# From the second block on, attention takes all four sequences of a block in one go

## The chip, the cores and the metric

One core of a Trainium2 chip runs one program. The metric is device time in microseconds (us). TensorE (PE) multiplies matrices; PEld is its loading of weights. VectorE (DVE), ScalarE (ACT) and GpSimd (POOL) do elementwise work, and SyncE (SP) issues nearly all transfers.

## The reference

A gated linear attention over 4 sequences, 8 heads and 768 positions feeds two MLPs, one behind the other. All is float32.

```
for c in range(nc):                              # chunks along the sequence
    L = exp(cum[i] - cum[j]) * causal            # decay inside the chunk
    M = einsum('bhin,bhjn->bhij', Cc, Bc) * L    # scores, weighed
    y[:, :, sl] = M @ xc + (Cc @ state) * exp(cum)
    state = decay_full * state + sum_j Bc x xc * decay_from_j
x = y as (4*768 tokens, 256)
x = softplus(x @ w_in) @ w_out                   # 256 -> 2048 -> 256
out = act2(x @ w2_in) @ w2_out                   # 256 -> 2048 -> 256
```

## The kernel before

**Blocks and units.** The kernel cuts the sequence into 6 blocks of 128 positions (c = 0 to 5), and a block into 4 units, one for each sequence (u = 4c to 4c+3). Blocks 1 to 5 are worked pair by pair: units 4c and 4c+1, then 4c+2 and 4c+3. A pair has these jobs, named as in the code, with a job's number being that of the last unit (scores: of the pair):

- rows, load, load_bc (SP): the clipped decays (tile ld), the inputs (u) and the operands of the scores (bc) are fetched. The buffers of rows and load are given back by the pair's out.
- decay (DVE, L1069): a scan along ld. sources (L1077) makes bt from u and ld; cd (L1089) scales u.
- scores (PE, L1104): 16 small products into four PSUM banks, two called y and two called acc.
- weigh (DVE, L1118): ld = scores * ld, four products of 128x256 a pair.
- st (PE, L1172 and L1150): the first half of ld times u, and the state's sums. Both go to the two y banks.
- carry (DVE, L1160) and sm (ACT, L1241): the new state and its copy that PE reads.
- out (PE, L1204 and L1172): the state's share, and the other half of ld times u.
- evac (ACT, L1224) and ready (DVE, L1232): the result goes as a high and a low part (xh, xl) to the MLP's input.

**The MLP.** Tokens go through layer 1 block by block in steps of 128 hidden columns: up (PE, L1262 to L1264, 3 products for each of 2 halves), g (ACT), g_hi (ACT or DVE), g_lo (DVE or POOL, L1372), down (PE, L1398, 6 matmuls into two acc banks). The first few downs are plain float32 (L1386). Each weight is split into a high and a low part before its first use (w0 to w3, w_hi, split_w: tiles wih, wil, woh, wol), mostly on DVE; some low parts and some g_lo are made on POOL. Blocks 4 and 5 of layer 1 (group 0) and all of layer 2 (groups 1 to 3) share products over two blocks: quads of jobs p15, p26, p37 and p4 on PE (L1269 to L1271), of which each waits for one result of ACT or DVE: fork (ACT) between p15 and p26, add1 (DVE) between p26 and p37, add2 (DVE) between p37 and p4.

**The order.** No engine chooses at run time. `program()` lists jobs with costs, due times and buffers, `Jobs.order` puts them into one list by a greedy rule, and each engine runs its jobs in that order. Constants (LAG_1, CHUNK, HASTE, BIAS) and a table (RUSH) shift due times and tie-breaks, so that a changed cost or constant moves jobs all over the program.

Of the kernel before, what the change touches and what calls it, by code (L numbers as in the profile page):

```python
# [14 lines left out]
NB, H, S, D, N = 4, 8, 768, 32, 16  # L15
# [12 lines left out]
class Jobs:  # L28
# [18 lines left out]
    def order(self, slots, begin):  # L47
# [53 lines left out]
        for _ in range(len(jobs)):  # L101
            best = []
            for name in ready:
# [10 lines left out]
            start, _, _, name, engine, got = min(  # L114
                (b for b in best if b[4] == first[4] and b[0] <= first[0] + (PATIENCE if first[0] > EARLY else HASTE)), key=lambda b: (b[1], b[0], b[2])
            )
# [96 lines left out]
def program():  # L213
# [38 lines left out]
    for u in range(NU):  # L252
# [24 lines left out]
        else:  # L277
            add(("sources", u), DVE, 210, needs=[("load", u)] + decay, takes=["bt"])
        if b % 2:
            v = u // 2  # L280
            add(
                ("scores", v), PE, 830 if c else 1270, needs=[("load_bc", v)] + (decay + [("decay", u - 1)] if c else [("scores", v - 1)] * v),
                takes=["y", "y", "acc", "acc"] if c else ["y", "y"] + [("acc", "h")] * 2 if v == 0 else [("h", "acc")] * 4,
                gives=[("load_bc", v)],
            )
        for hg in range(2):
            n = 2 * u + hg
            weighed = [("decay", u, hg), ("sources", u, hg)] if c == 0 else decay + [("sources", u)]

            bank = [("part", ("scores", u // 2), b % 2 * 2 + hg)]  # L290
            if n in WEIGH_POOL:
                add(("copy", u, hg), ACT, 490, needs=[("scores", u // 2)], takes=["g"], gives=bank)
                add(("weigh", u, hg), POOL, 1350, needs=weighed + [("copy", u, hg)], gives=[("copy", u, hg)])
            else:
                add(("weigh", u, hg), DVE, 340 if c else 600, needs=weighed + [("weigh", u, 0)] * hg + [("scores", u // 2)], gives=bank)
        both = [u] if c == 0 else [u - 1, u]
        if c == 0 or b % 2:

            needs = [("weigh", i, hg) for i in both for hg in range(2)] + ([("out", both[0] - 1)] if u else [])
            if c > 0:  # L300
                add(
                    ("st", u), PE, 990, needs=needs + [("sm", u - NB)], takes=["y", "y"], gives=[("sources", i) for i in both],
                )
                add(("carry", u), DVE, 300, needs=[("st", u), ("dec", c)])
                add(("sm", u, 1), ACT, 500, needs=[("carry", u)])
                needs = [("st", u), ("sm", u, 1)] + [("cd", i) for i in both]
# [5 lines left out]
            needs = [("out", u)]  # L312
            if c > 1:
                needs += [("split_w", 0, kind, j) for kind in "io" for j in range(8) if place_of(kind, j) == c]
                needs += [("down", s) for s in range(WHOLE)]
            if c == 1:

                needs += [("w2" if signed(0, kind, SX) else "w3", 0, kind, SX) for kind in "io"]
            due = when(first_step[c, b] - LEAD if c < 2 else min(first_step[c, b] - LEAD, CHUNK * (c - 1) + SPACE * b + SHIFT))
            add(("evac", u), ACT, 490 if c else 420, needs=needs)  # L320
            add(
                ("ready", u), DVE, 610 + 300 * (c < NC - 1) if c else 340, due=due, needs=[("evac", u)],
                gives=[("st", u) if c else ("out", u)] + [("dec", c)] * (b == NB - 1 and c > 0),
            )
# [81 lines left out]
    for s, (m, c, t0, n, fc, m_fc) in enumerate(steps):  # L406
# [102 lines left out]
BIAS_2 = 9000  # L509
# [6 lines left out]
LAG = 1500  # L516
LAG_1 = 6000
LAG_2 = 18000
# [7 lines left out]
RUSH = {  # L526
    ("cd", 6): -2000, ("columns", 1): -2000, ("decay", 2, 1): 16000, ("down", 1): -1000, ("down", 11): -4000,
    ("down", 2): -16000, ("down", 3): -16000, ("evac", 0): -4000, ("load_w", 0, "o", 3): -2000, ("load_w", 0, "o", 6): -16000,
    ("split_w", 0, "i", 1): 16000, ("split_w", 0, "o", 5): 2000, ("w0", 0, "o", 0): 1000, ("w0", 0, "o", 4): 1000,
    ("w1", 0, "o", 3): -2000, ("w3", 0, "i", 2): -8000, ("w3", 0, "i", 5): 16000, ("w3", 0, "o", 6): -16000,  # L530
    ("w_hi", 0, "i", 1): 1000, ("weigh", 0, 1): -2000,
# [8 lines left out]
def tile_kernel(ctx: ExitStack, tc: tile.TileContext, a0, al, bc, ub, w_in, w_out, w2_in, w2_out, out):  # L540
# [46 lines left out]
    def join():  # L587

        assert jobs.start["out", NB - 1] < jobs.start["scores", NB // 2]
# [501 lines left out]
    def cb_t(u, hg):  # L1091
        return buf(*got["scores", u // 2][u % 2 * 2 + hg])

    @job
    def scores(engine, v):

        t = mine("load_bc", v)[0]
# [30 lines left out]
    def y_t(u):  # L1128
# [4 lines left out]
        buf("y", 0)  # L1133
        i = u % 2
        return bufs["pair"][:, :, i * Q:i * Q + Q], None

    def states_t(u, s):
        buf("y", 0)
        return bufs["pair"][:, s, 256:384].rearrange("p (i n) -> p i n", i=2)

    @job
    def st(engine, u):

        intra_turn(u, 0)
        for i in range(2):
            x, bt = parts(u - 1 + i)[0], flat(bt_t(u - 1 + i))
            for p in range(4):
                for s in range(2):
                    r, o = slice(s * HALF, s * HALF + HALF), slice(p * 32, p * 32 + 32)
                    nc.tensor.matmul(  # L1150
                        states_t(u, s)[o, i], bt[r, p * 32:p * 32 + 32], x[r, p * 64:p * 64 + 64], start=False, stop=True,
                        skip_group_check=True,
                    )
# [24 lines left out]
    def intra_turn(u, turn):  # L1178

        for i in (u - 1, u):  # L1180
            for h in range(4):
                for s in range(2):
                    intra(i, (s + turn) % 2 * 4 + h, halves[s], halves[s], turn == 0 and i == u - 1)

    def out_unit(engine, u):
        c, b = divmod(u, NB)
        if c == 0:
# [9 lines left out]
            return  # L1197
        for i in (u - 1, u):
            y, cdt = y_t(i)[0], parts(i)[2]
            for s in range(2):  # L1200
                for p in range(4):

                    r, o = slice(p * 32, p * 32 + 32), p % 2 * 64
                    nc.tensor.matmul(  # L1204
                        y[o:o + 64, p // 2, halves[s]], sm_t[b // 2][s][r, i % 2], cdt[r, halves[s]], start=False,
                        stop=False, skip_group_check=True,
# [5 lines left out]
    def columns_of(c, b):  # L1212

        n, o = (Q, b * Q) if c == 0 else (2 * Q, b * Q - Q)
        y = y_t(b)[0] if c == 0 else bufs["pair"][:, :, 0:n]
        return [y] + [t[c][:, :, o:o + n] for t in (xh, xl)]
# [207 lines left out]
    with tc.manual_schedule():  # L1424
# [106 lines left out]
```

## Time and profile before

| | |
|---|---|
| median of 3 runs | 564.5 us (563.31 to 564.63) |
| profiled execution | 563.84 us, span 561.9 us, clock share of PE 0.998 |
| PE busy | 553.3 us, 98% of the span |
| PE weight loads | 445.4 us, 79% |
| DVE busy | 449.9 us, 80% |
| ACT busy | 385.1 us, 69% |
| POOL busy | 27.6 us, 5% |
| chain that ended last | PE 91%, DVE 4%, DMA 2% |
| fetch of a pair's decays (ld<-clip_z) | 20 of 256 KB, median 4.6 us to landing |

The busy time of an engine is an average over the whole span. In a row of the timeline the first number is the start in us from the span's start, the second how long the row lasted; a row with xN holds N equal instructions.

### The profile page before, as it was taken

Reading aid. Unit: us, or ns where it says so; the run is one execution under the profiler, and the core shown is the slowest. Engines: PE = TensorE matmul, PEld = TensorE weight load, DVE = VectorE, ACT = ScalarE, POOL = GpSimd, SP = SyncE. Lnnn points to the kernel's source line nnn. Section 1 sums busy time; section 2 is a strip of 40 time slices with the busy share of each in tenths; the row PEclk is TensorE's granted clock in tenths of the full one; section 3 lists DMA queues with packets and bytes.
Section 4 is the critical chain, followed back from the end, with each engine's and each line's share of the span. In section 5 each row is a group of like instructions: output and inputs, shape, how many; then the busy total and the mean of one; then the engine's idle time right before and its main releaser. Section 6 shows DMA issues by size and latency. Waiting matters only on the chain.

```text
span 561.9 us, 10574 instructions
## 1 busy us (share of the span) xinstructions
PE 553.3 (98%) x4070; PEld 445.4 (79%) x4070; DVE 449.9 (80%) x841; ACT 385.1 (69%) x706; POOL 27.6 (5%) x34
## 2 busy tenths in 40 slices
PE   9899999999999999999999999999999999999997
PEld 4767898777778888788888788788788888888885
DVE  6899976687896899877897999967976665876664
ACT  6977744445555666756657887886787785777873
POOL 4030300000000100000100000200100000000000
PEclk9999999999999999999999999999999999999999
DMA  8986541658445003578847132103200001000002
GB/s 283 389 225 187 157 118 31 196 171 225 119 149 178 0 2 93 214 237 304 275 142 240 59 118 90 56 6 108 76 0 1 0 1 38 37 1 0 1 1 76
DMA packets 34679, 64.74 MB, mean 115 GB/s; under 512 B 3684, under 2 KB 8164, under 8 KB 34628
## 3 DMA queue, kind: packets, MB, share of 16 engines
q1 hardware_dynamic: 34628, 64.06, 35.3%
q8 instruction: 32, 0.52, 0.4%
q14 instruction: 19, 0.16, 0.1%
HBM read 47.61 MB, written 16.43 MB: 114 GB/s over the span
## 4 chain that ended last, share of the span: by engine, by line
PE 91%; DVE 4%; DMA 2%; ACT 1%; SPq 1%; issue 1%; DVEq 0%; ACTq 0%
PE acc L1398 44%; PE h L1262 5%; PE h L1269 4%; PE h L1263 4%; PE h L1264 4%; PE h L1271 4%; PE h L1270 4%; PE z L1269 4%; PE z L1271 4%; PE z L1270 4%; PE y L1172 2%; DMA st<-in_w_out_dram 2%; PE acc L1386 1%; PE y L1204 1%; PE y L1104 1%
## 5 line engine op out<-in xcount | busy, mean ns | idle before, releaser
L1372 DVE TENSOR_TENSOR gl<-g,gh 128x512 fp32r<-128x512 f32 x184 | 126.5, 692 | 51.3 <-PE acc L1398 35.4
L1398 PE MATMUL acc<-gh,woh 128*128 128x512 f32 (+1 forms) x384 | 148.9, 390 | 0.0
L1398 PE MATMUL acc<-gh,wol 128*128 128x512 f32 (+1 forms) x384 | 146.5, 384 | 0.0
L683 ACT CAST gh<-g 128x512 fp32r<-128x512 f32 x155 | 96.1, 620 | 32.2 <-PE acc L1398 18.4
L1398 PE MATMUL acc<-gl,woh 128*128 128x512 f32 (+1 forms) x384 | 115.1, 383 | 0.0
L1398 PEld LDWEIGHTS acc<-gh,woh 128*128 128x128 f32 x384 | 72.1, 188 | 16.1 <-issue 1.2
L1398 PEld LDWEIGHTS acc<-gh,wol 128*128 128x128 f32 x384 | 72.2, 188 | 13.5 <-DVE wol L916 0.2
L1398 PEld LDWEIGHTS acc<-gl,woh 128*128 128x128 f32 x384 | 70.9, 188 | 14.4
L1357 ACT ACTIVATE g<-h 128x512 f32<-128x512 f32 x65 | 38.7, 595 | 56.2 <-PE h L1264 41.3
L1349 ACT ACTIVATE t<-t 128x512 f32<-128x512 f32 x96 | 60.8, 634 | 1.9
L1262 PE MATMUL h<-xh,wih 128*128 128x512 f32 (+1 forms) x130 | 48.5, 373 | 0.0
L1263 PE MATMUL h<-xh,wil 128*128 128x512 f32 (+1 forms) x130 | 46.6, 358 | 0.7 <-DVE wil L916 0.7
L1264 PE MATMUL h<-xl,wih 128*128 128x512 f32 (+1 forms) x130 | 46.3, 356 | 0.0
L1263 PEld LDWEIGHTS h<-xh,wil 128*128 128x128 f32 x130 | 24.5, 189 | 4.8 <-DVE wil L916 1.1
L1069 DVE TENSOR_TENSOR_SCAN ld<-ld,eye_t 128x512 f32<-128x512 f32 x20 | 25.8, 1326 | 3.2 <-DMA ld<-clip_z 3.2
L1262 PEld LDWEIGHTS h<-xh,wih 128*128 128x128 f32 x130 | 24.5, 189 | 4.5 <-issue 0.4
L1264 PEld LDWEIGHTS h<-xl,wih 128*128 128x128 f32 x130 | 24.5, 189 | 3.6
L1342 ACT ACTIVATE t<-h 128x512 f32<-128x512 f32 x37 | 22.1, 597 | 7.6 <-PE h L1271 6.0
L1361 DVE TENSOR_TENSOR g<-h,t 128x512 f32<-128x512 f32 x37 | 25.3, 684 | 1.8 <-ACT t L1349 0.8
L1361 DVE TENSOR_TENSOR g<-z,t 128x512 f32<-128x512 f32 x35 | 23.8, 683 | 1.5 <-ACT t L1349 0.8
L1342 ACT ACTIVATE t<-z 128x512 f32<-128x512 f32 x35 | 20.9, 596 | 5.5 <-PE z L1271 3.2
L1322 DVE TENSOR_TENSOR dec_plain<-h,dec_plain 128x512 f32<-128x512 f32 x22 | 15.1, 688 | 7.8 <-PE h L1271 7.6
(321 smaller groups left out, 1004.2 us busy)
## 6 DMA issues: line engine op xcount, KB each, us to landing
st<-in_w_in_dram SPq DMA_DIRECT2D x15, 512.0 KB, 4.0
st<-in_w_out_dram SPq DMA_DIRECT2D x15, 512.0 KB, 4.2
u<-in_ub_dram SPq DMA_DIRECT2D x24, 256.0 KB, 5.5
ld<-clip_z SPq DMA_DIRECT2D x20, 256.0 KB, 4.6
bc<-in_bc_dram SPq DMA_DIRECT2D x12, 384.0 KB, 7.9
pre_i<-st_plain SPq DMA_DIRECT2D x14, 256.0 KB, 3.6
pre_o<-st_plain SPq DMA_DIRECT2D x12, 256.0 KB, 3.7
pre_s<-st_plain SPq DMA_DIRECT2D x14, 192.0 KB, 4.0
```

The lines of the kernel that those rows point to most:

```text
L683: nc.scalar.copy(out, in_)
L1262: nc.tensor.matmul(o, wh, xh[c][:, k, t0:t0 + n], start=(k == 0), stop=False)
L1263: nc.tensor.matmul(o, wl, xh[c][:, k, t0:t0 + n], start=False, stop=False)
L1264: nc.tensor.matmul(o, wh, xl[c][:, k, t0:t0 + n], start=False, stop=(k == 1))
L1269: nc.tensor.matmul(bank, wh, bh, start=start, stop=False, skip_group_check=True)
L1270: nc.tensor.matmul(bank, wl, bh, start=False, stop=False, skip_group_check=True)
L1271: nc.tensor.matmul(bank, wh, bl, start=False, stop=True, skip_group_check=True)
L1342: nc.scalar.activation(out=t, in_=ph, func=act_funcs.IDENTITY_SAT240, scale=SAT)
L1349: nc.scalar.activation(out=t, in_=t, func=AF.Square, scale=0.5 / SAT, bias=0.5)
L1361: nc.vector.tensor_tensor(out=g, in0=ph, in1=t, op=ALU.max)
L1372: engines[engine].tensor_tensor(out=mine("g_lo", s)[0], in0=mine("g", s)[0], in1=mine("g_hi", s)[0].bitcast(F32), op=ALU.subtract)
L1398: nc.tensor.matmul(acc_t(s, e), w, g[:, j * n:(j + 1) * n], start=(begins(e, j) and g is gh and i == 0), stop=(fc + j == NFC - 1 and g is ...
```

## The change

With TOGETHER = (1, 2, 3, 4, 5), blocks 1 to 5 no longer go pair by pair. One scores job computes both pairs, the second into the other half of the same four banks. One st job holds the half products of all four units and the state sums of both pairs, the latter in two acc banks, since y now holds the outputs of four units. One out job follows. Every matmul, every weigh, carry, sm, evac and ready stays, on the same shapes. The buffers of ld and u of all four units are held until that one out, so the next block's rows and loads are issued after it. bt has four buffers in place of three. LAG_1 makes the downs of group 0 due later, and CHUNK, HASTE, BIAS, STAND_BY and RUSH are new numbers for the order.

```diff
+def units_of(u):
+
+    c = u // NB
+    return [u] if c == 0 else list(range(NB * c, NB * c + NB)) if c in TOGETHER else [u - 1, u]
...
-        if b % 2:
+        both = units_of(u)
+        n_pairs = len(both) // 2
+        if u == both[-1] and b % 2:
             v = u // 2
+            pairs = [v - 1, v] if n_pairs == 2 else [v]
             add(
-                ("scores", v), PE, 830 if c else 1270, needs=[("load_bc", v)] + (decay + [("decay", u - 1)] if c else [("scores", v - 1)] * v),
+                ("scores", v), PE, 200 + 630 * n_pairs if c else 1270,
+                needs=[("load_bc", i) for i in pairs] + ([("decay", i) for i in both[:2]] if c else [("scores", v - 1)] * v),
...
-                    ("st", u), PE, 990, needs=needs + [("sm", u - NB)], takes=["y", "y"], gives=[("sources", i) for i in both],
+                    ("st", u), PE, 200 + 790 * n_pairs, needs=needs + [("sm", i - NB) for i in both[1::2]],
+                    takes=["y", "y"] + ["acc", "acc"] * (n_pairs == 2), gives=[("sources", i) for i in both],
...
-                ("out", u), PE, 1220 if c else 750, needs=needs, takes=["y"] * (c == 0),
-                gives=[("load", i) for i in both] + [("rows", u) if c else ("part", ("spread", u, 0), 1)]
+                ("out", u), PE, 200 + 1010 * n_pairs if c else 750, needs=needs, takes=["y"] * (c == 0),
+                gives=[("load", i) for i in both] + ([("rows", i) for i in both[1::2]] if c else [("part", ("spread", u, 0), 1)])
...
+TOGETHER = (1, 2, 3, 4, 5)
+BT = 4
...
-BIAS = {DVE: 200, POOL: 2200}
+BIAS = {DVE: 300, POOL: 2200}
...
-HASTE = 200
-CHUNK = 8
+HASTE = 100
+STAND_BY = 400
+FAR = 40000.0
+CHUNK = 10
...
-LAG_1 = 6000
+LAG_1 = 9000
...
     def intra_turn(u, turn):
 
-        for i in (u - 1, u):
+        for i in units_of(u):
             for h in range(4):
                 for s in range(2):
-                    intra(i, (s + turn) % 2 * 4 + h, halves[s], halves[s], turn == 0 and i == u - 1)
+                    intra(i, (s + turn) % 2 * 4 + h, halves[s], halves[s], turn == 0 and i == units_of(u)[0])
```

Two places show the new order. On PE, the out of block 1 stood before as two jobs; this is the first, between a down and an up (u are the inputs of a unit, sm the state's copies, ld the weighed decays; x8 are equal matmuls in a row):

```order
L1398 MATMUL acc_266<-gl,woh_93 128x512
L1204 MATMUL y<-u_129,sm_140 64x64 x4
L1204 MATMUL y<-u_129,sm_141 64x64 x4
L1204 MATMUL y<-u_130,sm_140 64x64 x4
L1204 MATMUL y<-u_130,sm_141 64x64 x4
L1172 MATMUL y<-ld_121,u_129 32x64 x8
L1172 MATMUL y<-ld_121,u_130 32x64 x8
L1262 MATMUL h_207<-xh_375,wih_78 128x512
```

The same place in the changed kernel:

```order
L1242 MATMUL y<-u_129,sm_140 64x64 x4
L1242 MATMUL y<-u_129,sm_141 64x64 x4
L1242 MATMUL y<-u_130,sm_140 64x64 x4
L1242 MATMUL y<-u_130,sm_141 64x64 x4
L1242 MATMUL y<-u_131,sm_142 64x64 x4
L1242 MATMUL y<-u_131,sm_143 64x64 x4
L1242 MATMUL y<-u_132,sm_142 64x64 x4
L1242 MATMUL y<-u_132,sm_143 64x64 x4
L1210 MATMUL y<-ld_121,u_129 32x64 x8
L1210 MATMUL y<-ld_121,u_130 32x64 x8
L1210 MATMUL y<-ld_120,u_131 32x64 x8
L1210 MATMUL y<-ld_120,u_132 32x64 x8
```

One job of 64 small matmuls stands where there were two jobs of 32 with ups and downs between them; the same holds for each scores and each st. On DVE, the weighs of the first pair of block 2 (units 8 and 9, ahead of st 9) stood before like this (gl: g_lo, woh: w_hi of a weight, s: carry; a scan is listed as SCALAR_TENSOR_TENSOR):

```order
L1372 TENSOR_TENSOR gl<-g,gh 128x512
L685 CAST woh_96<-w_855 128x512
L1118 TENSOR_TENSOR ld_121<-y,ld_121 128x256
L1118 TENSOR_TENSOR ld_121<-acc_286,ld_121 128x256
L1118 TENSOR_TENSOR ld_121<-y,ld_121 128x256
L1118 TENSOR_TENSOR ld_121<-acc_268,ld_121 128x256
L1069 SCALAR_TENSOR_TENSOR ld_120<-ld_120,eye_t 128x512 x2
L1160 SCALAR_TENSOR_TENSOR s_66<-s_66,dec_134,y 128x64 x2
L1077 TENSOR_TENSOR bt_304<-u_131,ld_120 128x128
```

In the changed kernel the last six weighs of block 2 (of eight, units 8 to 11, ahead of st 11), and what follows them up to wil_88, the low part of a weight that up 14 needs:

```order
L1153 TENSOR_TENSOR ld_120<-y,ld_120 128x256
L1153 TENSOR_TENSOR ld_120<-acc_286,ld_120 128x256
L1153 TENSOR_TENSOR ld_121<-y,ld_121 128x256
L1153 TENSOR_TENSOR ld_121<-acc_268,ld_121 128x256
L1153 TENSOR_TENSOR ld_121<-y,ld_121 128x256
L1153 TENSOR_TENSOR ld_121<-acc_286,ld_121 128x256
L806 SCALAR_TENSOR_TENSOR w_685<-st_135,w_685 128x512
L1117 TENSOR_TENSOR u_129<-u_129,dec_134 128x128
L1117 TENSOR_TENSOR u_130<-u_130,dec_134 128x128
L1117 TENSOR_TENSOR u_131<-u_131,dec_134 128x128
L1117 TENSOR_TENSOR u_132<-u_132,dec_134 128x128
L944 TENSOR_TENSOR wil_88<-w_685,wih_80 128x512
```

Both pairs' weighs now stand in one row, behind both pairs' scans. Counted over DVE's whole order, from the start to the last weigh of unit 9 before and to the last weigh of unit 11 now: scans 6 and 8, sources 6 and 8, weighs 20 and 24, cd 6 and 4, g_lo 7 and 2, split_w 10 and 11, w2 16 and 15, w3 11 and 10; the other kinds even out. POOL has nine long jobs up to there in the changed kernel (split_w of two weights, g_lo of steps 6 to 9, one split_w, g_lo of steps 12 and 13). PE's order up to st 9 before and up to st 11 now has: two scores of two pairs in place of three of one, one st of two pairs in place of two, one out of two pairs in place of two, and downs 12 and 13 in place of ups 14 and 15. In the quads, the number of places where only one down (6 matmuls) stands between a product and the next one that waits for its result goes from 9 of 24 to 23 of 24 in group 0, and from 54 to 66 of 144 over all groups.

## Rows read from the trace of the kernel before

**Rows 1.** Busy time of each engine in two stretches (us, instructions; granted clock, DMA)

```profile
45.00:71.80 26.80, 26.80 (x433) 21.26 (x419) 26.80 (x55) 18.62 (x38) 6.09 (x4) 1.00 0.60 174
71.80:92.00 20.20, 20.20 (x248) 18.32 (x248) 14.06 (x28) 10.04 (x20) 0.00 (x0) 1.00 0.22 63
```

**Rows 2.** Timeline of PE around a scores, an st and an out

```profile
103.37 0.39 PE L1264 MATMUL h<-xl,wih 128*128 128x512 f32 x1
103.69 0.34 PE L1104 MATMUL y<-bc 32*64 32x128 f32 x4
...
104.09 0.29 PE L1104 MATMUL acc<-bc 32*64 32x128 f32 x4
...
104.88 0.39 PE L1398 MATMUL acc<-gh,woh 128*128 128x512 f32 x1
...
106.94 0.39 PE L1264 MATMUL h<-xl,wih 128*128 128x512 f32 x1
107.26 0.45 PE L1172 MATMUL y<-ld,u 64*32 64x64 f32 x32
107.53 0.59 PE L1150 MATMUL y<-u,bt 64*32 64x64 f32 x32
...
108.61 0.40 PE L1398 MATMUL acc<-gh,woh 128*128 128x512 f32 x1
...
110.68 0.39 PE L1264 MATMUL h<-xl,wih 128*128 128x512 f32 x1
110.99 0.69 PE L1204 MATMUL y<-u,sm 32*64 32x64 f32 x32
111.62 0.45 PE L1172 MATMUL y<-ld,u 64*32 64x64 f32 x32
...
112.58 0.40 PE L1398 MATMUL acc<-gh,woh 128*128 128x512 f32 x1
```

**Rows 3.** Groups of PE from 92 to 174 us (busy us, mean ns)

```profile
L1172 PE MATMUL y<-ld,u 64*32 64x64 f32 x448 | 6.4, 222 | 0.0
```

**Rows 4.** Timeline of PE at st 9

```profile
71.77 0.46 PE L1172 MATMUL y<-ld,u 64*32 64x64 f32 x32
```

**Rows 5.** Timeline of DVE, 28 to 73 us

```profile
28.93 1.65 DVE L916 TENSOR_TENSOR wil<-w,wih 128x512 fp32r<-128x512 f32 x1
...
36.24 3.37 DVE L1069 TENSOR_TENSOR_SCAN ld<-ld,eye_t 128x512 f32<-128x512 f32 x2
...
63.40 0.68 DVE L1372 TENSOR_TENSOR gl<-g,gh 128x512 fp32r<-128x512 f32 x1
64.00 0.68 DVE L778 SCALAR_TENSOR_TENSOR w<-st,w 128x512 uint32<-128x512 uint32 x1
...
69.93 0.41 DVE L1118 TENSOR_TENSOR ld<-acc,ld 128x256 f32<-128x256 f32 x1
70.26 2.32 DVE L1069 TENSOR_TENSOR_SCAN ld<-ld,eye_t 128x512 f32<-128x512 f32 x2
```

**Rows 6.** Timeline of POOL: the first and the last of 7 pieces from 20 to 71 us

```profile
27.07 2.96 POOL L916 TENSOR_TENSOR wol<-w,woh 128x512 fp32r<-128x512 f32 x2 [12.91 <-ACT woh L683]
...
69.09 1.30 POOL L916 TENSOR_TENSOR wol<-w,woh 128x512 fp32r<-128x512 f32 x1 [9.07 <-DVE woh L685]
```

**Rows 7.** DMA issues from 23 to 30 us (number, KB each, median us to landing)

```profile
ld<-clip_z SPq DMA_DIRECT2D x4, 256.0 KB, 9.6
```

**Rows 8.** Whom PE waited for, whole span (us in total, times, longest)

```profile
PE h L1269 <- DVE h L1312: 0.3, 1, 0.3
PE z L1269 <- ACT h L1297: 0.3, 1, 0.3
PE h L1269 <- DVE dec_plain L1322: 0.2, 1, 0.2
```

**Rows 9.** Timeline of PE from 228 to 234 us: the first of these waits

```profile
230.78 0.61 PE L1398 MATMUL acc<-gl,woh 128*128 128x512 f32 x2
231.69 0.50 PE L1269 MATMUL h<-xh,ld_later 128*128 128x512 f32 x1 [0.29 <-DVE h L1312]
```

More of the change, by code (lines that the diff above doesn't have):

```diff
@@ L114, in order @@
             start, _, _, name, engine, got = min(
-                (b for b in best if b[4] == first[4] and b[0] <= first[0] + (PATIENCE if first[0] > EARLY else HASTE)), key=lambda b: (b[1], b[0], b[2])
+                (b for b in best if b[4] == first[4] and b[0] <= first[0] + (
+                    STAND_BY if b[1] + FAR < first[1] else PATIENCE if first[0] > EARLY else HASTE
+                )), key=lambda b: (b[1], b[0], b[2])
             )
@@ L195, in whole, with last_of @@
     return s < WHOLE
+def units_of(u):
+    c = u // NB
+    return [u] if c == 0 else list(range(NB * c, NB * c + NB)) if c in TOGETHER else [u - 1, u]
+def last_of(u):
+    return units_of(u | 1)[-1] if u // NB not in TOGETHER else u // NB * NB + NB - 1
 def pair_of(u):
@@ L278, in program @@
             add(("sources", u), DVE, 210, needs=[("load", u)] + decay, takes=["bt"])
-        if b % 2:
+        both = units_of(u)
+        n_pairs = len(both) // 2
+        if u == both[-1] and b % 2:
             v = u // 2
+            pairs = [v - 1, v] if n_pairs == 2 else [v]
             add(
-                ("scores", v), PE, 830 if c else 1270, needs=[("load_bc", v)] + (decay + [("decay", u - 1)] if c else [("scores", v - 1)] * v),
+                ("scores", v), PE, 200 + 630 * n_pairs if c else 1270,
+                needs=[("load_bc", i) for i in pairs] + ([("decay", i) for i in both[:2]] if c else [("scores", v - 1)] * v),
                 takes=["y", "y", "acc", "acc"] if c else ["y", "y"] + [("acc", "h")] * 2 if v == 0 else [("h", "acc")] * 4,
-                gives=[("load_bc", v)],
+                gives=[("load_bc", i) for i in pairs],
             )
@@ L288, in program @@
             weighed = [("decay", u, hg), ("sources", u, hg)] if c == 0 else decay + [("sources", u)]
-            bank = [("part", ("scores", u // 2), b % 2 * 2 + hg)]
+            seen = ("scores", last_of(u) // 2)
+            early = n_pairs == 2 and b < 2
+            bank = [("part", seen, b % 2 * 2 + hg)] * (not early)
             if n in WEIGH_POOL:
-                add(("copy", u, hg), ACT, 490, needs=[("scores", u // 2)], takes=["g"], gives=bank)
+                add(("copy", u, hg), ACT, 490, needs=[seen], takes=["g"], gives=bank)
                 add(("weigh", u, hg), POOL, 1350, needs=weighed + [("copy", u, hg)], gives=[("copy", u, hg)])
             else:
-                add(("weigh", u, hg), DVE, 340 if c else 600, needs=weighed + [("weigh", u, 0)] * hg + [("scores", u // 2)], gives=bank)
-        both = [u] if c == 0 else [u - 1, u]
-        if c == 0 or b % 2:
+                before = [("weigh", u, 0)] * hg + [("weigh", u - 2, hg)] * (n_pairs == 2 and not early)
+                add(("weigh", u, hg), DVE, 340 if c else 600, needs=weighed + before + [seen], gives=bank)
+        if u == both[-1] and (c == 0 or b % 2):
             needs = [("weigh", i, hg) for i in both for hg in range(2)] + ([("out", both[0] - 1)] if u else [])
@@ L301, in program @@
                 add(
-                    ("st", u), PE, 990, needs=needs + [("sm", u - NB)], takes=["y", "y"], gives=[("sources", i) for i in both],
-                )
-                add(("carry", u), DVE, 300, needs=[("st", u), ("dec", c)])
-                add(("sm", u, 1), ACT, 500, needs=[("carry", u)])
-                needs = [("st", u), ("sm", u, 1)] + [("cd", i) for i in both]
-            add(
-                ("out", u), PE, 1220 if c else 750, needs=needs, takes=["y"] * (c == 0),
-                gives=[("load", i) for i in both] + [("rows", u) if c else ("part", ("spread", u, 0), 1)]
+                    ("st", u), PE, 200 + 790 * n_pairs, needs=needs + [("sm", i - NB) for i in both[1::2]],
+                    takes=["y", "y"] + ["acc", "acc"] * (n_pairs == 2), gives=[("sources", i) for i in both],
+                )
+                for i in both[1::2]:
+                    add(("carry", i), DVE, 300, needs=[("st", u), ("dec", c)])
+                    add(("sm", i, 1), ACT, 500, needs=[("carry", i)])
+                needs = [("st", u)] + [("sm", i, 1) for i in both[1::2]] + [("cd", i) for i in both]
+            add(
+                ("out", u), PE, 200 + 1010 * n_pairs if c else 750, needs=needs, takes=["y"] * (c == 0),
+                gives=[("load", i) for i in both] + ([("rows", i) for i in both[1::2]] if c else [("part", ("spread", u, 0), 1)])
                 + [("sources", u, 0)] * (c == 0),
             )
-            needs = [("out", u)]
+        if c == 0 or b % 2:
+            end = last_of(u) if c else u
+            needs = [("out", end)]
             if c > 1:
@@ L318, in program @@
                 needs += [("w2" if signed(0, kind, SX) else "w3", 0, kind, SX) for kind in "io"]
+            if c and u == end and n_pairs == 2:
+                needs += [("ready", u - 2)]
             due = when(first_step[c, b] - LEAD if c < 2 else min(first_step[c, b] - LEAD, CHUNK * (c - 1) + SPACE * b + SHIFT))
@@ L322, in program @@
                 ("ready", u), DVE, 610 + 300 * (c < NC - 1) if c else 340, due=due, needs=[("evac", u)],
-                gives=[("st", u) if c else ("out", u)] + [("dec", c)] * (b == NB - 1 and c > 0),
+                gives=([("st", u)] * (u == end) if c else [("out", u)]) + [("dec", c)] * (b == NB - 1 and c > 0),
             )
@@ L526 @@
 RUSH = {
[L527 to L530, printed above, removed]
+    ("columns", 1): -2000, ("decay", 2, 1): 16000, ("down", 122): -16000, ("down", 148): 8000, ("down", 2): -16000,
+    ("g_lo", 6): -8000, ("p26", 24): -8000, ("p4", 22): -16000, ("split_w", 0, "i", 1): 16000, ("up", 27): -4000,
     ("w_hi", 0, "i", 1): 1000, ("weigh", 0, 1): -2000,
@@ L587, in join @@
     def join():
-        assert jobs.start["out", NB - 1] < jobs.start["scores", NB // 2]
+        assert len(of_pair) == 1
         for i in range(2):
@@ L1091, in cb_t, with scores_of @@
     def cb_t(u, hg):
-        return buf(*got["scores", u // 2][u % 2 * 2 + hg])
+        bank = buf(*got["scores", last_of(u) // 2][u % 2 * 2 + hg])
+        return bank[:, 256:512] if u // NB in TOGETHER and u % NB > 1 else bank
     @job
     def scores(engine, v):
+        if v % 2 and 2 * v // NB in TOGETHER:
+            scores_of(v - 1)
+        scores_of(v)
+    def scores_of(v):
         t = mine("load_bc", v)[0]
@@ L1144, in st @@
         intra_turn(u, 0)
-        for i in range(2):
-            x, bt = parts(u - 1 + i)[0], flat(bt_t(u - 1 + i))
+        for i in units_of(u):
+            x, bt = parts(i)[0], flat(bt_t(i))
             for p in range(4):
@@ L1150, in st @@
                     nc.tensor.matmul(
-                        states_t(u, s)[o, i], bt[r, p * 32:p * 32 + 32], x[r, p * 64:p * 64 + 64], start=False, stop=True,
-                        skip_group_check=True,
+                        states_t(i | 1, s)[o, i % 2], bt[r, p * 32:p * 32 + 32], x[r, p * 64:p * 64 + 64],
+                        start=u // NB in TOGETHER and i % NB == 0, stop=True, skip_group_check=True,
                     )
@@ L1197, in out_unit @@
             return
-        for i in (u - 1, u):
+        for i in units_of(u):
             y, cdt = y_t(i)[0], parts(i)[2]
@@ L1204, in out_unit @@
                     nc.tensor.matmul(
[L1205 removed]
+                        y[o:o + 64, p // 2, halves[s]], sm_t[i % NB // 2][s][r, i % 2], cdt[r, halves[s]], start=False,
                         stop=False, skip_group_check=True,
@@ L1214, in columns_of @@
         n, o = (Q, b * Q) if c == 0 else (2 * Q, b * Q - Q)
-        y = y_t(b)[0] if c == 0 else bufs["pair"][:, :, 0:n]
+        first = o if c in TOGETHER else 0
+        y = y_t(b)[0] if c == 0 else bufs["pair"][:, :, first:first + n]
         return [y] + [t[c][:, :, o:o + n] for t in (xh, xl)]
@@ L1470, in tile_kernel @@
             got[name] = slots
-            if name == ("scores", NB // 2):
+            if name[0] == "scores" and 2 * name[1] >= NB and len(of_pair) == 1:
                 join()
+            assert name[0] not in ("scores", "out") or len(of_pair) == 1 or name[1] >= NB // 2
             kind, args = (name[0], name[1:]) if isinstance(name, tuple) else (name, ())
```

8 lines of the change are left out of this document (6 added, 2 removed).

## Prediction

> **What bounds the kernel now.** I read the busy times by stretch first [rows 1], then PE's timeline around the small matmuls [rows 2 to 4], then DVE and POOL in the same stretch [rows 5, 6]. From 45 us to the end PE is busy nearly without a break, so from there the time is the sum of what PE issues, plus the few waits that the view of waits shows [rows 8]. A full matmul starts 0.23 us after the one before it. [rows 1] show two more things: DVE is full too from 45.00 to 71.80 (26.80 of 26.80 us), and no longer after that (14.06 of 20.20). So a saving on PE before 72 us is only paid out if DVE is ready for it; a later one is paid at once.
>
> **What a switch to the small matmuls costs.** Each call in [rows 2] is read from the last full matmul before it to the third matmul after it, less three steps of 0.23, because the second matmul after a call starts late too, by some 0.1.
> - scores: 104.88 - 103.37 - 0.69 = 0.82. Its 32 starts reach from 103.69 to about 104.11, so 32 more in the same job cost 0.43, and a job less saves 0.39.
> - st: 108.61 - 106.94 - 0.69 = 0.98. The first piece takes 0.27, the second 0.59 less one matmul of 0.22 [rows 3], so a second pair costs 0.64 and the merged job saves 0.34.
> - out: 112.58 - 110.68 - 0.69 = 1.21. Here 0.16 lies between its two pieces (110.99 + 0.69 - 0.22 = 111.46 to 111.62), which a merged job pays once. A second pair costs 0.74, so 0.47 is saved.
>
> That is 1.20 us a block and 6.0 us over five blocks. PE keeps all its other matmuls. Inside a job the operands already change from unit to unit every 8 or 16 matmuls and the starts stay about 10 ns apart, so I cost the join of the two pairs at nothing; if it cost as much as the break inside an out (0.16), four joins a block (one in scores, one in each of the pieces of st and out, less one) would take 0.6 a block, 3 us in all.
>
> **What DVE makes of it.** The merged jobs ask for all four units' weighs at once. I compare the same point of PE's order: before st 9, which began at 71.77 [rows 4], and now st 11, the first st for which DVE has to hurry. PE's own work up to there changes by +0.04 (two scores of 1.25 for three of 0.82), -0.34 (one st) and -0.47 (one out), and downs 12 and 13 stand for ups 14 and 15 of the same length: -0.77, so PE could be there at 71.0.
>
> DVE could not. Up to its last weigh before st 9 it ended at 69.93 + 0.41 = 70.34 [rows 5], without an idle stretch. Up to the last weigh of unit 11 it now has two more scans (2.32 for two), four more weighs (0.33 each, 69.93 to 70.26), two more sources against two fewer cd of the same shape, one split_w more, one w2, one w3 and five g_lo fewer (six less, at 0.60 from 63.40 to 64.00): 2.32 + 1.32 - 3.60 = 0.04. So in plain prices DVE does the same work as before.
>
> What is not the same is POOL, to which the g_lo went. It had 7 pieces up to there [rows 6] and now has 9. DVE is slower beside a POOL piece: a split took 1.65 in place of 0.68 at 28.93, two scans 3.37 in place of 2.32 [rows 5], so about 1.0 for a piece. The weighs beside the last piece (69.09 to 70.39) kept their 0.41. I take 2.0 for two more pieces: st 11 at 70.34 + 0.04 + 2.0 + 0.1 = 72.5. The bounds: 70.5 if they fall beside weighs, and then PE's 71.0 decides; 75.4 if the two new ones hold DVE for their whole length (1.48 each, 2.96 for two in the first of [rows 6]) and two that were free before are not free any more (1.0 each).
>
> The Trainium skill has a rule for this: in "SBUF — State Buffer", section "Who interferes with whom", a DVE instruction with two SBUF inputs and a GpSimd instruction that reads SBUF take turns, and the later one is fully blocked. The weighs, with one input in PSUM, agree with it, the split loses 1.0 and not 1.48. By the rule in full st 11 would come at 73.5, an estimate from that page, and the time 1.0 later than mine.
>
> Behind the weighs DVE's next rows are w3, four cd and then wil_88, which up 14 needs right after st 11, while st 11 covers 1.6 of it. I put 0.3 for this wait (0 to 1.0).
>
> **The sum**, against the profiled execution of 563.84: 72.5 at st 11, plus what was left before, 563.84 - 71.77 = 492.07, less the scores of the pair that is done already (0.82), less the merges still to come (3 x 0.39 + 4 x 0.34 + 4 x 0.47 = 4.41), plus 0.3: **559.6**. That is 4.2 us or 0.7% less than the profiled execution, which itself lies 0.7 under the median of 564.5 and within the runs shown. I forecast 559.8.
>
> **Costed at nothing.** The new start order (an up earlier, other weights first) moves PE before 45 us; what it gives or takes there is swallowed by DVE's end at 72.5. The later downs of group 0 and the tighter quads: PE does the same matmuls, and as long as the products' results come in one down's time (1.36) it does not wait; before, PE's three waits there came to 0.8 [rows 8]. If the cover goes, each late result costs about 0.45 (in [rows 9] the next start was due at 230.78 + 2 x 0.23 = 231.24 and came at 231.69). The fetch of block 3 to 5's decays comes later, after the merged out, but some 15 us of ups and downs lie ahead of their scores. carry and sm of two pairs must fit under the 12 matmuls (2.72) between st and out: two carries, one sm and the signals make about 2.0.
>
> **The rivals.**
> - **DVE keeps up.** The POOL pieces fall beside weighs or other work that does not care, and PE decides: st 11 at 71.0 or a little under, all 6.0 saved but the 0.3: 557.5 to 558.1. For it: the last of the old pieces cost the weighs beside it nothing [rows 5, 6]. Against: the split and the scans paid about 1.0 for one.
> - **Block 2's fetch is late.** The buffers of ld are given back by the out of block 1, by my count at about 56 us in place of 51 for the first pair before. With a usual landing of 4.6 us and 2.6 for issuing four fetches, the scans could begin at 61 to 63, just when DVE comes to them (about 63). When the DMA engines were full a fetch took 9.6 [rows 7]: then scans, weighs and st 11 come 3 to 5 later, 563 to 564.5: no change. The upper bound of POOL's cost ends at the same time. For it: the first st's second pair now also waits for its fetch. Against: the DMA engines are not full there.
> - **The quads stall (slower).** 23 places of group 0 now have one down as their only cover. At 0.45 each, from 13 such stalls on the saving is lost, and with all 23 (10.3 us less the 0.8 of before) the time is about 569. Against: before, of 54 such places no more than three showed a wait.
> - **The join costs what a switch costs**, so the change does not do what it says: 563 to 564.
>
> **The numbers.** About 0.3% (1.7 us) is what a measurement of this kernel can tell from no change. Forecast (558.3 to 562.7) 0.54, DVE keeps up 0.22, late fetch or POOL's upper bound or a costly join (562.8 to 566) 0.18, quads stall 0.06. Faster: 0.54 + 0.22 = 0.76; same 0.18; slower 0.06. The range from 557.2 to 563.2 holds the forecast, nearly all of the second and about a third of the third case.
>
> **What would show it.** Right: 64 starts in one scores row group, and a distance from the last up to the third matmul after it of 1.94 (1.25 + 0.69); DVE full up to about 72 and st 11 waiting for its last weigh there; 110 us on, PE ahead by about 4. Wrong: st 11 before 71 (the second case), DVE idle before a scan at 61 to 66 (late fetch), or waits of PE for fork, add1 or add2 that sum to over 2 us between 215 and 300.

## The result and the profile after

| | before | after |
|---|---|---|
| median (lowest to highest) | 563.9 us (562.86 to 564.63) | 559.13 us (557.96 to 559.83) |
| ratio, 95% interval | | 0.9915 (0.9893 to 0.9937) |
| profiled execution, span | 563.84, 561.9 us | 559.83, 558.1 us |

The kernel is 4.8 us (0.85%) faster; the forecast was 559.8. A second set of runs on another chip gave 0.9912 (0.9888 to 0.9937).

The timeline of PE around the joined calls of block 4 answers to [rows 2]:

```profile
123.52 0.61 PE L1437 MATMUL acc<-gl,woh 128*128 128x512 f32 x2
124.07 0.34 PE L1139 MATMUL y<-bc 32*64 32x128 f32 x4
...
124.33 0.29 PE L1139 MATMUL y<-bc 32*64 32x128 f32 x4
...
124.44 0.29 PE L1139 MATMUL y<-bc 32*64 32x128 f32 x4
...
124.55 0.32 PE L1139 MATMUL y<-bc 32*64 32x128 f32 x4
...
125.20 0.50 PE L1437 MATMUL acc<-gh,woh 128*128 128x512 f32 x1
125.54 0.40 PE L1437 MATMUL acc<-gh,wol 128*128 128x512 f32 x1
125.78 0.39 PE L1437 MATMUL acc<-gh,woh 128*128 128x512 f32 x1
...
128.96 0.61 PE L1437 MATMUL acc<-gl,woh 128*128 128x512 f32 x2
129.51 0.80 PE L1210 MATMUL y<-ld,u 64*32 64x64 f32 x60
...
131.49 0.40 PE L1437 MATMUL acc<-gh,woh 128*128 128x512 f32 x1
...
133.55 0.39 PE L1303 MATMUL h<-xl,wih 128*128 128x512 f32 x1
133.87 1.16 PE L1242 MATMUL y<-u,sm 32*64 32x64 f32 x64
134.96 0.88 PE L1210 MATMUL y<-ld,u 64*32 64x64 f32 x64
...
136.34 0.39 PE L1437 MATMUL acc<-gh,woh 128*128 128x512 f32 x1
```

Read as before, from the last full matmul to the third after the call, less 0.69 (a row with x2 holds its second start 0.23 after the first): scores 125.78 - 123.75 - 0.69 = 1.34, st 131.49 - 129.19 - 0.69 = 1.61, out 136.34 - 133.55 - 0.69 = 2.10. Together 5.05 against 2 x 3.01 = 6.02 for two pairs: a block saves 0.97, where 1.20 was forecast.

The missing 0.23 is not a pause at the seam between the two pairs. In the scores the second pair begins at 124.55, 0.11 after the last group of the first pair (124.44), as that group began 0.11 after its own predecessor (124.33). The loss lies in the starts of the second pair: in the out, the first 32 matmuls of L1210 start within 0.24 (134.96 to 135.19), the last 32 within 0.43 (135.19 to 135.62). Why the later ones start further apart no run shows.

Now DVE ahead of st 11, with POOL and then PE at the same time (answering to [rows 4 to 6]):

```profile
61.66 0.46 DVE L1198 SCALAR_TENSOR_TENSOR s<-s,dec,acc 128x64 f32<-128x64 f32 x2
63.11 6.67 DVE L1097 TENSOR_TENSOR_SCAN ld<-ld,eye_t 128x512 f32<-128x512 f32 x4 [0.99 <-DMA ld<-clip_z]
...
72.48 0.41 DVE L1153 TENSOR_TENSOR ld<-y,ld 128x256 f32<-128x256 f32 x1
72.81 0.41 DVE L1153 TENSOR_TENSOR ld<-acc,ld 128x256 f32<-128x256 f32 x1
```

```profile
63.47 4.12 POOL L1411 TENSOR_TENSOR gl<-g,gh 128x512 fp32r<-128x512 f32 x2 [1.17 <-issue]
```

```profile
71.65 0.28 PE L1303 MATMUL h<-xl,wih 128*128 128x256 f32 x1
72.94 0.80 PE L1210 MATMUL y<-ld,u 64*32 64x64 f32 x60 [1.01 <-DVE ld L1153]
...
74.52 0.49 PE L1301 MATMUL h<-xh,wih 128*128 128x512 f32 x1
75.28 0.50 PE L1302 MATMUL h<-xh,wil 128*128 128x512 f32 x1 [0.27 <-DVE wil L944]
```

The four scans wait 0.99 for their fetch and then take 6.67 in place of 2 x 2.32 = 4.64: 2.03 lost beside two POOL pieces. PE stands ready at about 71.9 and starts st 11 at 72.94. That is before the last weigh ends (73.22): st writes the y banks, in which the scores lie, and the seventh weigh, the last that reads a y bank, ends at 72.89. Whom PE waited for in the whole span:

```profile
PE y L1210 <- DVE ld L1153: 2.6, 2, 1.6
PE h L1468 <- DVE idle L1466: 1.1, 1, 1.1
PE z L1308 <- ACT h L1336: 0.8, 1, 0.8
PE h L1302 <- DVE wil L944: 0.8, 3, 0.3
```

The first row is st 7 (1.6) and st 11 (1.0); neither wait was there before. The third is a new wait of the quads, at 225 us. The view of before has, beside the rows of [rows 8] and the same 1.1 for the idle tile, these two, at 15.8 and 30.6 us:

```profile
PE y L1477 <- DVE xl L1232: 1.8, 1, 1.8
PE h L1263 <- DVE wil L916: 0.7, 1, 0.7
```

The date of st 11 differs between executions of the same order. In the profile of the second set it came at 72.89, but PE had waited only 0.6 at st 7 and 0.7 at st 11, and 1.4 for a fetch at the start. In that of the kernel split_late (below), which runs the same instructions in the same order on every engine up to 84 us, it came at 70.78: there less of POOL's work fell beside DVE instructions that it delays. What one profile shows of st 11 is therefore good to about 2 us.

### The profile page after: what moved, and what is told of

It reads as the page before. It is cut to its first block, busy times and chain, and to the rows that moved or that the text cites. A ratio compares the mean times of both kernels' runs of the same rounds, so it can differ in the third digit from the quotient of the medians.

```text
span 558.1 us, 10604 instructions
## 1 busy us (share of the span) xinstructions
PE 547.2 (98%) x4070; PEld 447.2 (80%) x4070; DVE 449.5 (81%) x833; ACT 387.0 (69%) x710; POOL 33.8 (6%) x38
## 4 chain that ended last, share of the span: by engine, by line
PE 78%; DVE 12%; DMA 3%; ACT 3%; issue 3%; SPq 0%; DVEq 0%
PE acc L1437 39%; PE h L1308 5%; PE h L1310 5%; PE h L1309 5%; PE z L1308 4%; PE z L1310 4%; PE z L1309 4%; PE h L1302 3%; PE h L1301 3%; PE h L1303 3%; DMA st<-in_w_out_dram 2%; DVE gl L1411 2%; DVE ld L1097 1%; PE y L1210 1%; DMA ld<-clip_z 1%
## 5 line engine op out<-in xcount | busy, mean ns | idle before, releaser
L1437 PE MATMUL acc<-gh,woh 128*128 128x512 f32 (+1 forms) x384 | 146.9, 385 | 0.0
L711 ACT CAST gh<-g 128x512 fp32r<-128x512 f32 x162 | 100.4, 620 | 20.0 <-PE acc L1437 11.6
L1381 ACT ACTIVATE t<-h 128x512 f32<-128x512 f32 x41 | 24.6, 600 | 16.3 <-PE h L1310 11.5
L1400 DVE TENSOR_TENSOR g<-h,t 128x512 f32<-128x512 f32 x41 | 28.0, 685 | 3.3 <-ACT t L1388 3.1
L1351 DVE TENSOR_TENSOR h<-h,dec_plain 128x512 f32<-128x512 f32 x20 | 14.0, 699 | 14.8 <-PE h L1310 14.8
L1361 DVE TENSOR_TENSOR dec_plain<-h,dec_plain 128x512 f32<-128x512 f32 x26 | 17.9, 689 | 7.7 <-PE h L1310 7.6
L1400 DVE TENSOR_TENSOR g<-z,t 128x512 f32<-128x512 f32 x31 | 21.2, 685 | 2.7 <-ACT t L1388 2.1
```

Source lines behind the costliest of these rows:

```text
L711: nc.scalar.copy(out, in_)
L1400: nc.vector.tensor_tensor(out=g, in0=ph, in1=t, op=ALU.max)
L1437: nc.tensor.matmul(acc_t(s, e), w, g[:, j * n:(j + 1) * n], start=(begins(e, j) and g is gh and i == 0), stop=(fc + j == NFC - 1 and g is ...
```

## The experiments

All times are medians; "before" ran on the same chip each time, and ratios to it are compared.

**1. Join and numbers apart.** Two kernels: joined with the old numbers, and the new numbers without the join.

```diff
 TOGETHER = (1, 2, 3, 4, 5)
...
-LAG_1 = 9000
+LAG_1 = 6000
...
```

> Blocks 1 to 5 joined as in the change, but with the numbers of before (LAG_1 6000, CHUNK 8, HASTE 200, BIAS 200, the old RUSH, no STAND_BY). Theory A (the joined calls themselves are the gain, some 1.2 us a block on PE; the numbers only trim the order): most of the gain stays, 558.5 to 561.5 us against 563.9 of before. Theory B (the new numbers are the gain: fewer waits in the quads, an earlier start, and the join gives little): 562.5 to 565.

```diff
-TOGETHER = (1, 2, 3, 4, 5)
+TOGETHER = ()
```

> The numbers of the changed kernel, but every block pair by pair (TOGETHER empty). Theory A: no gain that can be told from none, 562.5 to 566 us, and a scores, an st and an out cost PE 0.82, 0.98 and 1.21 us each again. Theory B: 558.5 to 560.5, as the change.

Measured: 575.77 us, 1.0219 (1.0184 to 1.0253), and 561.79 us, 0.9951 (0.9934 to 0.9968). Neither theory holds alone. The numbers without the join gain 2.7 us, and the join on top of them 2.0 (0.9951 less 0.9915, of 564; by the two intervals 2.0 give or take 1.6). The join with the old numbers loses 11. Most of that lies in the quads, which stall there: starts of full matmuls that come late after 222 us (counted as in the section on the prediction) sum to 9.5, against 2.7 before. The largest row of PE's waits stands for three of them:

```profile
PE h L1310 <- DVE h L1353: 4.2, 3, 2.5
```

DVE and POOL of the same kernel ahead of st 11 show another place of the loss:

```profile
62.93 7.72 DVE L1099 TENSOR_TENSOR_SCAN ld<-ld,eye_t 128x512 f32<-128x512 f32 x4 [0.22 <-DMA ld<-clip_z]
70.57 2.61 DVE L1107 TENSOR_TENSOR bt<-u,ld 128x128 f32<-128x128 f32 x2
```

```profile
63.30 1.95 POOL L946 TENSOR_TENSOR wil<-w,wih 128x512 fp32r<-128x512 f32 x1 [10.97 <-ACT wih L713]
65.20 7.83 POOL L1413 TENSOR_TENSOR gl<-g,gh 128x512 fp32r<-128x512 f32 x4
```

Here the order puts five POOL pieces beside the scans and the first two bt. They cost DVE 7.72 - 4.64 = 3.08 on the scans and 2.61 - 0.48 = 2.13 on the bt (0.48 as in the same rows elsewhere), 1.04 for each piece, and PE waits 3.0 at st 11.

**2. The later downs alone.** The change with `LAG_1 = 6000`.

> The change with LAG_1 at 6000 as before, nothing else. If the later downs of group 0 keep the quads fed: PE's waits for fork, add1 and add2 between 215 and 420 us grow from about 1.5 to 4 to 8 us, and the time is 562 to 567. If the lag only moves downs that PE does anyway: 558.5 to 560.

Measured: 561.23 us, 0.9940 (0.9917 to 0.9963), against 559.62 for the change on the same chip. PE's two waits in the quads are 0.9 and 0.6, against 0.8 and 0.2 in the change. The medians differ by 1.6, but the two intervals overlap; the late starts after 222 us differ by 1.0 (2.7 against 1.7). So the lag is worth some 1 us, a size that neither expectation gave; waits of 4 to 8 us did not come.

**3. POOL's pieces.** First the six g_lo that POOL makes ahead of st 11 go to DVE, at the same places of the order.

```diff
+        to_dve = {("g_lo", s) for s in (6, 7, 8, 9, 12, 13)}
+        order = [(name, DVE if name in to_dve else engine, slots) for name, engine, slots in order]
         for name, engine, slots in order:
...
```

> The change, with the six g_lo that POOL makes before 72 us (steps 6 to 9, 12, 13) given to DVE at the same places of the order. The theory of contention (a POOL piece of this kind costs DVE about 1.0 us, so DVE does them cheaper itself, at 0.6): the four scans of block 2 take 4.7 in place of 6.7, DVE's last weigh of block 2 comes 1.5 to 2.7 us sooner, PE's waits for weighs (1.6 at st 7 and 1.0 at st 11) shrink, and the time falls by 1.0 to 2.5, to 556.5 to 558. The rival (DVE has 3.6 us more of work and loses nothing otherwise; the long scans are the DMA's or something else): st 11 about 2 to 3.6 later, 561 to 563.

Measured: 559.12 us, 0.9901 (0.9877 to 0.9926), not told apart from the change. But the place moved as the theory of contention says. DVE's groups from 61 to 67 us:

```profile
L1097 DVE TENSOR_TENSOR_SCAN ld<-ld,eye_t 128x512 f32<-128x512 f32 x4 | 4.6, 1198 | 0.0
```

The same four scans take 4.6, where they took 6.67 or 6.68 in each profile of the change's own order (both sets, and split_late). PE has no wait for a weigh left, although DVE has 3.6 us more to do. St 11 begins at 71.80 in place of 72.94, but that alone would prove little, as said above. The gain was largely given back in PE's waits for those g_lo, at their unchanged places: 1.4 in two waits, and 1.2 in place of 0.8 for the fork at 225. So their places were mended too, in two steps:

```diff
+        to_dve = {("g_lo", s) for s in (6, 7, 8, 9, 12, 13)} | {("split_w", 0, "o", j) for j in (0, 1)}
...
+            (("g_lo", 8), ("split_w", 0, "o", 4)), (("g_lo", 9), ("carry", 7)), (("g_lo", 12), ("decay", 9)),
+            (("split_w", 0, "o", 0), ("split_w", 0, "o", 2)), (("split_w", 0, "o", 1), ("split_w", 0, "o", 0)),
+            (("a_hi", 7), ("fork", 16)),
...
```

> The change with eight of POOL's nine pieces before 72 us on DVE (the six g_lo and the first two split_w of the second weights), g_lo 8 and 9 moved behind the rows that PE needs sooner, g_lo 12 ahead of the last two scans, and on ACT the fork of quad 16 ahead of the a_hi of step 7. Theory of contention: no wait of PE for a weigh at st 7 and st 11, none of 1.0 for g_lo at 50 us, none of 1.0 for the fork at 225 us; st 11 at 70.5 to 71.5; 555.5 to 557 us. The rival (DVE loses as much as POOL gave up): 558.5 to 560.5.

Measured: 557.56 us (556.73 to 558.64) against 559.62 (558.62 to 562.28) for the change on the same chip; 0.9871 (0.9847 to 0.9895). St 11 begins at 70.80 and no wait for a weigh is left, as the theory of contention had it, but the time lies between the two ranges expected.

```diff
+        to_dve = {("g_lo", s) for s in (6, 7, 8, 9, 12, 13)} | {("split_w", 0, "o", j) for j in (0, 1)} | {("w_hi", 0, "o", 4)}
...
+            (("a_hi", 7), ("fork", 16)), (("add1", 16), ("p26", 16)),
...
```

> The tuned kernel (eight POOL pieces on DVE), with the w_hi of weight o 4 from ACT to DVE and, on DVE, the add1 of quad 16 ahead of the s_sum of step 4. By its trace PE's waits at 47.8 (0.5), 49.5 (0.7) and 225 (0.8) should go: 555.8 to 557.2 us. If the waits only move on: 557.2 to 558.5.

Measured: 555.86 us, 0.9852 (0.9829 to 0.9874): 8.3 us under before and 3.4 under the change (0.9913 as the mean of its two sets, times 564), the fastest kernel of the study. Whom PE waited for in it:

```profile
PE h L1468 <- DVE idle L1466: 1.1, 1, 1.1
PE y L1528 <- DVE xl L1271: 0.7, 1, 0.7
PE acc L1425 <- ACT gh L1396: 0.5, 1, 0.5
PE z L1308 <- DVE z L1351: 0.2, 1, 0.2
```

The first two are at the start, where the change has them too. The 2.6 for weighs are gone, and st 11 begins at 69.75. This kernel also gives a w_hi of ACT to DVE and moves two jobs of the quads (fork and add1 come sooner), so the 3.4 are not the price of POOL's pieces alone.

**4. The fetch.** The decays of block 2 go into two buffers that are idle since block 0, and are issued earlier.

```diff
+        order = list(order)
+        at = [o[0] for o in order].index(("load_w", 0, "i", 7))
+        early = [(("rows", 9), SP, [("ld", 0)]), (("rows", 11), SP, [("ld", 1)])]
+        order = order[:at] + early + [o for o in order[at:] if o[0] not in (("rows", 9), ("rows", 11))]
```

> The change, with the decays of block 2 fetched into two buffers that are idle since block 0, and some 6 us sooner in SP's order. If the fetch is what is late at 62 to 63 us (DVE idle for 0.99 there): that idle goes, st 11 begins about 1.0 sooner, at 71.9, where PE itself stands, and the time falls by 0.5 to 1.0, to about 558.3. If DVE's own work decides (the fetch only fills a gap that POOL's pieces would eat anyway): st 11 moves by under 0.3 and the time stays at 559.

Measured: 561.25 us, 0.9945 (0.9923 to 0.9967), slower than the change by 1.7 (the intervals overlap), and st 11 at 74.36. Neither expectation came true: DVE no longer waits for this fetch, but it comes there later. One place, on POOL and on ACT:

```profile
48.02 3.26 POOL L1411 TENSOR_TENSOR gl<-g,gh 128x512 fp32r<-128x512 f32 x1 [7.33 <-ACT gh L711]
```

```profile
51.30 0.60 ACT L1396 ACTIVATE g<-h 128x512 f32<-128x512 f32 x1 [2.91 <-POOL gl L1411]
```

A POOL piece took 3.26, where the same piece took 1.29 in the change; DVE worked without a gap beside it, from 48.05 to 50.13. ACT's g waited 2.91 for it, and behind that g stood the w_hi for which DVE then waited 1.65. So what the late fetch costs by itself stays open; the run shows the contention from POOL's side.

**5. Undoing the join block by block.** First by the constant, `TOGETHER = (3, 4, 5)`.

> TOGETHER = (3, 4, 5): blocks 1 and 2, for which DVE has to hurry, go pair by pair, with all other numbers as in the change. The theory that a join is paid out only where DVE is not late: as the run with all blocks pair by pair (561.8) less three joins of about 1.3 each, 557.5 to 558.5 us, a little better than the change, with no wait of PE for weighs before 75 us. The rival (each join is worth the same wherever it stands): two joins fewer than the change, 561 to 562.

Measured: 563.54 us, 0.9974 (0.9957 to 0.9991), outside both. The constant makes a new order everywhere: PE waits 1.6 for a g at 109 us and 0.9 for an add in the quads, which the change does not. That is no test of the join. So in the next runs the order is kept, and each joined call is only issued in two halves, around the PE job that stood before it.

```diff
...
+            if name[0] in ("scores", "st", "out") and name[1] // (NU // 2 // NC if name[0] == "scores" else NB) in (3, 4, 5):
+                p = max(i for i in range(n) if order[i][1] == PE)
+                order[p:n + 1] = order[p + 1:n] + [(name + ("first",), PE, slots), order[p], (name + ("second",), PE, slots)]
...
```

> The change with the order kept, but in blocks 3, 4 and 5 each scores, st and out is issued in two halves with the PE job that stood before it between them: nine more switches. If a switch costs PE what the rows say (scores 0.41, st 0.46, out 0.43 saved by a join): PE pays all nine, 3 x 1.3 = 3.9 us, and the time is 563 to 564. If the join is worth little here (the time sits in waits that move along): 559 to 561.

Measured: 563.25 us, 0.9979 (0.9964 to 0.9994): 3.7 us over the change, as the rows said. From st 11 to the last matmul its profile has 554.66 - 70.78 = 483.88, the change 553.19 - 72.94 = 480.25, so it takes 3.6 more. Its halved calls, read as above, cost 6.08 in block 5 (0.82 + 0.84 for scores, 1.00 + 0.99 for st, 1.22 + 1.21 for out), about 1.04 more than a joined block, so 3.1 for three blocks; one wait of 0.24 ahead of a half st comes on top, and the last 0.3 was not traced.

For blocks 1 and 2 the same edit has (1, 2) in place of (3, 4, 5):

> The same halving in blocks 1 and 2 alone. If DVE decides when st 7 and st 11 begin (PE waited 1.6 and 1.0 for weighs there): scores and st of both blocks and the out of block 1 are covered by those waits, and only the out of block 2 is paid, 0.4 to 1.0 us, 559.5 to 560.5. If a join is paid wherever it stands: 2 x 1.3 = 2.6, 562.

Measured: 563.86 us, 0.9996 (0.9981 to 1.0011): 4.7 over the change, more than either said. The theory of cover falls, for a reason that the timeline of PE and the windows around st 11 show:

```profile
74.02 0.68 PE L1215 MATMUL y<-ld,u 64*32 64x64 f32 x32 [2.37 <-DVE ld L1158]
```

```profile
72.00:74.00 2.00, 0.00 (x0) 0.00 (x0) 2.00 (x8) 0.00 (x0) 0.00 (x0) 0.91 0.00 2
74.00:75.00 1.00, 0.98 (x64) 0.94 (x64) 1.00 (x3) 0.07 (x1) 0.00 (x0) 0.50 0.00 0
75.00:76.00 1.00, 1.00 (x18) 0.87 (x5) 1.00 (x5) 0.54 (x1) 0.00 (x0) 0.50 0.00 0
76.00:77.00 1.00, 1.00 (x6) 1.00 (x6) 1.00 (x3) 0.00 (x0) 0.00 (x0) 0.50 0.00 0
77.00:78.00 1.00, 1.00 (x45) 0.87 (x47) 0.51 (x1) 0.24 (x1) 0.00 (x0) 0.98 0.06 16
```

The half st can't begin sooner than the whole one: it writes the y banks, which still hold the other pair's scores, so it waits for the same seventh weigh (73.97). But it stands a job earlier, and the up that covered a part of that wait now comes behind it. PE is idle for 2.4 us, and its granted clock then reads 0.50 (1.2 of 2.4 GHz) until 77. By the two profiles this kernel is 1.1 behind the change at st 11's start and 3.7 behind at the scores of block 3 (99.42 in place of 95.74). So 2.6 come behind that start, where the halved st and out and the slow clock stand together; they were not told apart.

> The kernel of the run before this one, with blocks 1 and 2 halved as above. In it PE has no wait for weighs at st 7 and st 11. If cover is what hid the halving in the other run, it is paid in full here: 2 x 1.3 = 2.6 us over the kernel it is made from. If the halving costs little for another reason: under 1.2 over it.

Measured: 559.59 us, 0.9915 (0.9894 to 0.9935): 3.7 over the kernel that it is made from (555.86). That is over the 2.6, but PE waits 2.8 for weighs here, where that kernel has no such wait: again a half st stands a job earlier than the whole one. So what the joins of blocks 1 and 2 are worth by themselves was not isolated.

## Why the prediction was right

The sum held (559.8 forecast, 559.1 measured), and so did its two main steps: a joined call saves PE a switch, and DVE beside POOL decides when st 11 begins. But the closeness is in part luck: errors of about 1 us cancelled. By the two profiles the time from the compared st to the end fell by 492.07 - (559.83 - 72.94) = 5.18. The forecast had 0.82 + 4.41 - 0.3 = 4.93 for this; the rows give 0.82 + 3.58 for the joins (0.30, 0.35 and 0.32 for a scores, an st and an out), 1.0 for the quads and 0.4 less for wil_88, which is 5.0. So the joins were put 0.8 too high and the quads 1.0 too low.

- **The joins.** Forecast 1.20 a block; the rows of block 4 give 0.97, and halving three blocks cost 3.6 to 3.7, 1.2 a block. The term mis-sized by the rows is the second pair inside a joined call. In the scores it costs 0.52 and not 0.43: the 0.43 reached only from the first to the last of 32 starts, without the step of 0.06 to the next pair. In the out it costs 0.89 and not 0.74, since its last matmuls start further apart. The rival "the join costs what a switch costs" asked for 0.6 a block; these are 0.24, and they are no pause at the join.
- **st 11.** Forecast 72.5, measured 72.94. By rows, DVE's instructions up to its last weigh lose 8.3 beside POOL's nine pieces, and lost 5.3 beside seven before: 3.0 more, not 2.0. The 1.0 for a piece was right. What was wrong is how many pieces cost nothing: about two of seven before, one of nine now. Then the fetch was late by 0.99, as the second rival had it, though for less than its 3 to 5. Against these: the start that I costed at nothing gave DVE about 1.0 less idle time before 45 us (5.2 in place of 6.2, worked out from its busy times 0 to 13.9 and 13.9 to 45), and st 11 began 0.3 before its last weigh was done, not 0.1 after. 72.5 + 1.0 + 1.0 - 1.0 - 0.4 = 73.1. That the two dates lie so close is luck as well, since the same order also gave 70.78 in another execution, where DVE lost 6.5 and not 8.3. Two readings of this step were off: st 7 waited too (1.6), though the prediction took st 11 for the first st for which DVE has to hurry, and PE stood ready at 71.9 and not at 71.0.
- **wil_88.** Forecast 0.3. The second matmul after a call starts 0.34 after the first (125.20 and 125.54 above), so the start due at 74.52 + 0.34 = 74.86 came at 75.28: 0.42.
- **The rule that I weighed.** In the Trainium skill, "SBUF — State Buffer", section "Who interferes with whom", a DVE instruction with two SBUF inputs and a GpSimd one that reads SBUF exclude each other. The scans (6.67 with two pieces, 4.6 without) agree, and a weigh, with one input in PSUM, took 0.41 beside a piece too. The rows show the two engines taking turns:

```profile
63.47 1.95 POOL L1411 TENSOR_TENSOR gl<-g,gh 128x512 fp32r<-128x512 f32 x1 [1.17 <-issue]
64.25 2.24 DVE L1097 TENSOR_TENSOR_SCAN ld<-ld,eye_t 128x512 f32<-128x512 f32 x1
65.38 2.21 POOL L1411 TENSOR_TENSOR gl<-g,gh 128x512 fp32r<-128x512 f32 x1
66.42 2.25 DVE L1097 TENSOR_TENSOR_SCAN ld<-ld,eye_t 128x512 f32<-128x512 f32 x1
```

  They end at 65.42, 66.49, 67.59 and 68.67, each 1.1 after the one before, on the other engine. So the loss is one turn, 1.0 to 1.1 for a piece, and not the 1.3 to 1.5 that a piece lasts by itself; the 73.5 that the rule gave in full and the 72.5 that I took lie on either side of 72.94.
- **The quads and the numbers.** I costed LAG_1 and the other numbers at nothing, and named stalls of the quads as a rival. They are what failed as a step: without any join they gain 2.7 us, and with the old numbers the join loses 11. Late starts of full matmuls after 222 us (what each start has over 0.23 after the one before, summed over PE's timeline) came to 2.7 before, 1.7 after, 0.6 with the new numbers alone and 9.5 with the join alone. So the rival of stalled quads is what came with the join and the old numbers; with the new numbers two waits showed.

So the join is worth 4.9 to 6 us on PE, but only with numbers that fit it; the two gains do not simply add. New waits in the change's profile stand against them (2.6 for weighs, 0.4 for wil_88, 0.8 at the fork), and the change got 4.8 in all. That more was to be had is shown by the kernel at 555.86.

## What to carry to other kernels

Where a call of small matmuls interrupts a stream of full ones, count the switches: here joining two calls saved 0.3 each, and it paid only as far as the engine that feeds the joined call was ready for all of it at once. Giving work to a second elementwise engine is no relief when its pieces exclude the first one's: price the piece by what it takes from the first engine (here 1.0) against what the first engine would need for it (here 0.6). Before a date in one profile is read as the effect of an edit, look at how far it moves between executions of one order: here st 11 moved by 2 us. And to test a part of a change in a scheduled kernel, edit the finished order; a constant of the scheduler moves jobs everywhere (blocks 3 to 5 alone by the constant gave 563.5, with new waits at 109 us and in the quads, far from the edit).

## What the runs showed of the hardware that was not expected

After idle stretches of 2.4 us (halved calls, up to 74 us), 2.3 us and 3.0 us (joined with the old numbers, up to 53 and 76 us) the granted clock of TensorE read 0.50 for about 3 us; after 1.6 and 1.0 us in the change it read 1.00 throughout. The length of the stretch alone does not tell it: in the kernel with the old numbers PE also waited 2.5 us up to 238.5, and the clock there stayed at 1.00. Between 75.5 and 76.8 in the halved kernel a matmul of half width (128x256) started every 0.21 us, and behind 77.1, at 1.00, every 0.12. POOL pays for the shared access as DVE does: the piece that took 1.29 in the change took 3.26 under a dense row of DVE instructions. And small matmuls in a long call do not keep the pace of the first ones: in the joined out, 32 of them start within 0.24 and the next 32 within 0.43.
